# Squared-ReLU attention, a 2-D Fourier mix and a feed-forward block on one core: the whole kernel rebuilt around paired heads, folded DFT sums and another order of issue

## The chip, the core and the metric

The kernel runs on 1 core of one Trainium2 chip. The metric is device time in microseconds (us) of one execution; lower is better. A core has one matrix engine (TensorE, PE in the profile; PEld is its loading of weights), a vector engine (VectorE, DVE), an activation engine (ScalarE, ACT), GpSimd (POOL) and SyncE (SP), which each work through their own queue of instructions in order, and 16 DMA engines that move data between DRAM and the on-chip memory SBUF. Matrix products land in PSUM, eight banks of 512 fp32 words per partition.

## The reference, cut to what matters

```python
# q, k, v: (8, 12, 448, 64)   w_ch1: (768, 3072)   w_ch2: (3072, 768)
scores = (1 / sqrt(64)) * q @ k.T                  # per batch and head: 448 x 448
attn   = maximum(scores, 0) ** 2 / 448
x      = (attn @ v), heads side by side            # (8, 448, 768)
mixed  = real(fft(fft(x, axis=1), axis=2))         # over tokens, then over channels
u      = x + mixed
un     = (u - mean(u)) / sqrt(var(u) + 1e-6)       # over the 768 channels
out    = u + maximum(un @ w_ch1, 0) @ w_ch2        # (8, 448, 768), fp32
```

## The kernel before, in words

The eight batches are worked through one after the other, by a Python loop over `b`. Tokens are cut into four chunks of 112 (`SC = 4`, `SP = 112`), channels into six of 128 (`MC = 6`), the hidden layer into 24 of 128 (`JC = 24`).

- Loads. `load_qkv` fetches q, k and v of a batch with 12 DMAs from GpSimd's queue, which also turn fp32 into bf16. The weights (30 DMAs, L120 and L125) are issued ahead of the first of them.
- `transpose_qk` turns q and k on TensorE (L97, L103); ACT and DVE copy the results out of PSUM.
- Attention. For each head and each key chunk: a score product (L146, 64 rows of the array), Relu on ACT into the tile `rsc`, of which there is one (L149), the square on DVE (L150), and the product with v (L153, 64 columns of the array). The output of a head is scaled into `xT` (L155).
- Fourier mix. `x` is turned back to rows (L164). The channel DFT uses full cosine and sine matrices over 385 of 768 output columns (L177, L181), the token DFT full 448-square ones (L191, L193); the other 383 columns follow by symmetry (L200, on GpSimd). `u` stays in SBUF.
- Normalisation and feed-forward. `un` is made per token chunk (L211 to L223), turned (L227), multiplied with w1 (L235, 448 tokens at a time), passed through Relu on ACT (L237), multiplied with w2 (L245, 112 tokens by 384 channels, 24 products to a sum), and added to `u` (L247).

Each engine's order is set by the Tile framework's scheduler, which interleaves what the program order and the tile buffers allow; a tile with `bufs=n` can be in use n times at once.

Of the kernel before, what the change touches and what calls it, by code (L numbers as in the profile page):

```python
# [8 lines left out]
FP32 = mybir.dt.float32  # L10
# [6 lines left out]
def build_dft(nc, pool, psum_pool, nrows, N, ncols, phase_num, zero_t, chunk=128, prefix='dft'):  # L17
    import math
    tiles = []
    nchunks = (nrows + chunk - 1) // chunk  # L20
    for ci in range(nchunks):
        p0 = ci * chunk
        p = min(chunk, nrows - p0)
        rowidx = pool.tile([p, 1], I32)
        nc.gpsimd.iota(rowidx, pattern=[[0, 1]], base=p0, channel_multiplier=1)
        rowf = pool.tile([p, 1], FP32)
        nc.vector.tensor_copy(rowf, rowidx)
        colidx = pool.tile([p, ncols], I32)
        nc.gpsimd.iota(colidx, pattern=[[1, ncols]], base=0, channel_multiplier=0)
        colf = pool.tile([p, ncols], FP32)  # L30
        nc.vector.tensor_copy(colf, colidx)
        prod = pool.tile([p, ncols], FP32)
        nc.vector.tensor_scalar(prod, colf, rowf, None, op0=ALU.mult)
        off = N // 4 if phase_num == 0 else 0
        y = pool.tile([p, ncols], FP32)
        nc.vector.tensor_scalar(y, prod, 1.0 / N, float(off) / N, op0=ALU.mult, op1=ALU.add)
        r = pool.tile([p, ncols], FP32)
        nc.vector.tensor_scalar(r, y, float(2 ** 23), None, op0=ALU.add)
        nc.vector.tensor_scalar(r, r, float(2 ** 23), None, op0=ALU.subtract)
        d = pool.tile([p, ncols], FP32)  # L40
        nc.vector.tensor_tensor(d, y, r, op=ALU.subtract)
        t = pool.tile([p, ncols], BF16, name=f'{prefix}_{ci}')
        nc.scalar.activation(t, d, AF.Sin, bias=zero_t[:p], scale=2.0 * math.pi)
        tiles.append(t)
    return tiles
# [3 lines left out]
def kernel(  # L49
# [13 lines left out]
    SC = 4  # L63
    SP = S // SC
    MC = D // 128
    JC = FF // 128
    NC2 = 385
# [4 lines left out]
    attn_pool = ctx.enter_context(tc.tile_pool(name="attn", bufs=1))  # L72
    psum = ctx.enter_context(tc.psum_pool(name="ps", bufs=1))

    q_nat = [attn_pool.tile([SP, D], BF16, name=f'qn{_i}') for _i in range(SC)]
    k_nat = [attn_pool.tile([SP, D], BF16, name=f'kn{_i}') for _i in range(SC)]
    v_nat = [attn_pool.tile([SP, D], BF16, name=f'vn{_i}') for _i in range(SC)]
    qT_all = [attn_pool.tile([128, S], BF16, name=f'qT{_i}') for _i in range(MC)]
    kT_all = [attn_pool.tile([128, S], BF16, name=f'kT{_i}') for _i in range(MC)]

    def load_qkv(b):
        for c in range(SC):
            sl = slice(c * SP, (c + 1) * SP)
            nc.gpsimd.dma_start(out=q_nat[c].rearrange('p (h d) -> p h d', h=H),
                                in_=q[b, :, sl, :].rearrange('h p d -> p h d'))
            nc.gpsimd.dma_start(out=k_nat[c].rearrange('p (h d) -> p h d', h=H),
                                in_=k[b, :, sl, :].rearrange('h p d -> p h d'))
            nc.gpsimd.dma_start(out=v_nat[c].rearrange('p (h d) -> p h d', h=H),  # L88
                                in_=v[b, :, sl, :].rearrange('h p d -> p h d'))

    def transpose_qk():
        for c in range(SC):
            sl = slice(c * SP, (c + 1) * SP)
            for m in range(MC):
                msl = slice(m * 128, (m + 1) * 128)
                pt = psum.tile([128, SP], BF16, tag='p0', bufs=2)
                nc.tensor.transpose(pt, q_nat[c][:, msl], ident[:SP, :SP])  # L97
                if m % 2 == 0:
                    nc.scalar.activation(qT_all[m][:, sl], pt, AF.Copy)
                else:  # L100
                    nc.vector.tensor_copy(qT_all[m][:, sl], pt)
                pt2 = psum.tile([128, SP], BF16, tag='p1', bufs=2)
                nc.tensor.transpose(pt2, k_nat[c][:, msl], ident[:SP, :SP])  # L103
                if m % 2 == 0:
                    nc.vector.tensor_copy(kT_all[m][:, sl], pt2)  # L105
                else:
                    nc.scalar.activation(kT_all[m][:, sl], pt2, AF.Copy)

    ident = const.tile([128, 128], BF16)
    make_identity(nc, ident)  # L110
    import math as _m
    zero_t = const.tile([128, 1], FP32)
    nc.gpsimd.memset(zero_t, 0.0)
    eps_t = const.tile([128, 1], FP32)
    nc.gpsimd.memset(eps_t, 1e-6)

    w1_sb = []
    for m in range(MC):
        t = wpool.tile([128, FF], BF16, name=f'w1_{m}')
        nc.gpsimd.dma_start(out=t, in_=moe_w_ch1[m * 128:(m + 1) * 128, :])  # L120
        w1_sb.append(t)
    w2_sb = []
    for j in range(JC):
        t = wpool.tile([128, D], BF16, name=f'w2_{j}')
        nc.gpsimd.dma_start(out=t, in_=moe_w_ch2[j * 128:(j + 1) * 128, :])  # L125
        w2_sb.append(t)

    CD = build_dft(nc, const, psum, D, D, NC2, 0, zero_t, prefix='CD')
    SD = build_dft(nc, const, psum, D, D, NC2, 1, zero_t, prefix='SD')
    CS = build_dft(nc, const, psum, S, S, S, 0, zero_t, chunk=SP, prefix='CS')  # L130
    SS = build_dft(nc, const, psum, S, S, S, 1, zero_t, chunk=SP, prefix='SS')

    load_qkv(0)
    transpose_qk()

    for b in range(B):
        xT = [work.tile([128, S], BF16, name=f'xT{_i}') for _i in range(MC)]
        attnT = [attn_pool.tile([SP, S], BF16, name=f'attnT{_i}') for _i in range(SC)]
        for h in range(H):
            mt = h // 2  # L140
            rof = (h % 2) * Dh
            qT_h = qT_all[mt][rof:rof + Dh, :]
            kT_h = kT_all[mt][rof:rof + Dh, :]
            for c in range(SC):
                ps_sc = psum.tile([SP, S], FP32, tag='p2', bufs=2)
                nc.tensor.matmul(ps_sc, lhsT=kT_h[:, c * SP:(c + 1) * SP], rhs=qT_h,  # L146
                                 start=True, stop=True)
                r = attn_pool.tile([SP, S], BF16, name='rsc')
                nc.scalar.activation(r, ps_sc, AF.Relu, scale=1.0 / 8.0)  # L149
                nc.vector.tensor_tensor(attnT[c], r, r, op=ALU.mult)  # L150
            ps_ao = psum.tile([Dh, S], FP32, tag='p3', bufs=2)
            for kc in range(SC):
                nc.tensor.matmul(ps_ao, lhsT=v_nat[kc][:, h * Dh:(h + 1) * Dh],  # L153
                                 rhs=attnT[kc], start=(kc == 0), stop=(kc == SC - 1))
            nc.scalar.activation(xT[mt][rof:rof + Dh, :], ps_ao, AF.Copy, scale=1.0 / S)  # L155

        if b + 1 < B:
            load_qkv(b + 1)

        x_nat = [attn_pool.tile([SP, D], BF16, name=f'xnat{_i}') for _i in range(SC)]  # L160
        for c in range(SC):
            for m in range(MC):
                pt = psum.tile([SP, 128], BF16, tag='p0', bufs=2)
                nc.tensor.transpose(pt, xT[m][:, c * SP:(c + 1) * SP], ident)  # L164
                if m % 2 == 0:
                    nc.scalar.activation(x_nat[c][:, m * 128:(m + 1) * 128], pt, AF.Copy)
                else:
                    nc.vector.tensor_copy(x_nat[c][:, m * 128:(m + 1) * 128], pt)

        A_sb = [work.tile([SP, NC2], BF16, name=f'Asb{_i}') for _i in range(SC)]  # L170
        B_sb = [work.tile([SP, NC2], BF16, name=f'Bsb{_i}') for _i in range(SC)]
        for c in range(SC):
            nsl = slice(c * SP, (c + 1) * SP)
            psA = psum.tile([SP, NC2], FP32, tag='p2', bufs=2)
            psB = psum.tile([SP, NC2], FP32, tag='p3', bufs=2)
            for m in range(MC):
                nc.tensor.matmul(psA, lhsT=xT[m][:, nsl], rhs=CD[m],  # L177
                                 start=(m == 0), stop=(m == MC - 1))
            nc.scalar.activation(A_sb[c], psA, AF.Copy)
            for m in range(MC):  # L180
                nc.tensor.matmul(psB, lhsT=xT[m][:, nsl], rhs=SD[m],  # L181
                                 start=(m == 0), stop=(m == MC - 1))
            nc.scalar.activation(B_sb[c], psB, AF.Copy)
# [20 lines left out]
        if b + 1 < B:  # L204
            transpose_qk()
# [73 lines left out]
```

## Time and profile before

| | |
|---|---|
| median of 3 runs | 1318.64 us (1317.91 to 1319.39) |
| the profiled execution, its span | 1317.1 us |
| instructions | 13229 |
| mean granted TensorE clock | 0.795 of full speed |
| read from DRAM, written | 51.90 MB, 11.01 MB |

The profiled execution lasted as long as its span, from the first instruction to the last; what lies around the span is the 1.5 us between it and the median. A line of the profile's groups reads: line of the kernel, engine, operation, output <- input by the program's names, partitions x elements and type, count | busy us, mean ns of one | idle us of the engine just before them, and what ended most of it. Durations of matrix products include their way through the array; the distance between the starts of two is what a stream of them costs.

### The profile page before, as it was taken

How to read it: one execution, taken by the hardware profiler on the slowest of the kernel's cores; microseconds unless marked ns; L12 is line 12 of the kernel's file. 1: busy time of each engine (PE TensorE's matmuls, PEld its weight loads, DVE VectorE, ACT ScalarE, POOL GpSimd, SP SyncE). 2: the span in 40 equal slices, each digit the busy share in tenths (PEclk: the TensorE clock that was granted, in tenths of full speed). 3: DMA queues.
4: the chain of work that ended last, by engine and by line, in shares of the span. 5: the costliest groups of instructions: out<-in, count | busy, mean ns of one | idle time of the engine just before them, and what ended most of it. 6: DMA issues, size and time to landing. Idle time of an engine off the chain costs nothing.

```text
span 1317.1 us, 13229 instructions
## 1 busy us (share of the span) xinstructions
PE 1134.0 (86%) x4864; PEld 582.0 (44%) x4864; DVE 414.9 (31%) x1196; ACT 529.2 (40%) x1302; POOL 171.1 (13%) x238
## 2 busy tenths in 40 slices
PE   0139979998899979999799988999799997999698
PEld 0012436525473345624365254733456244642456
DVE  0694340235113360133402351133601334023501
ACT  0236552364415543164423644055431645236440
POOL 3740120003000130001200030001300010000100
PEclk9999969857796569957698577965699576975799
DMA  9980360105410360103601063103601030000001
GB/s 188 151 53 1 21 43 11 32 1 38 26 31 11 22 43 0 43 0 21 43 11 31 0 41 23 32 11 21 43 1 42 0 22 0 14 30 0 1 1 42
DMA packets 137505, 37.82 MB, mean 29 GB/s; under 512 B 131552, under 2 KB 134624, under 8 KB 137440
## 3 DMA queue, kind: packets, MB, share of 16 engines
q0 software_dynamic: 137440, 36.97, 26.2%
q8 instruction: 38, 0.62, 0.2%
q14 instruction: 27, 0.22, 0.1%
HBM read 51.90 MB, written 11.01 MB: 48 GB/s over the span
## 4 chain that ended last, share of the span: by engine, by line
PE 71%; DVE 10%; issue 8%; ACT 5%; DMA 3%; POOL 2%; POOLq 0%; ACTq 0%
PE pch L245 17%; PE ph L235 16%; PE ps_sc L146 13%; PE ps_ao L153 12%; PE psB L181 3%; PE psA L177 3%; DMA w<-in_moe_w_ch_dram 3%; ACT rsc L149 3%; DVE usb L202 2%; PE pt L164 2%; PE pt L227 2%; POOL usb L200 2%; DVE attnT L150 2%; PE pt L97 2%; DVE Qsb L198 1%
## 5 line engine op out<-in xcount | busy, mean ns | idle before, releaser
L149 ACT ACTIVATE rsc<-ps_sc 112x448 bf16<-112x448 f32 x384 | 208.1, 542 | 360.9 <-PE ps_sc L146 219.3
L245 PE MATMUL pch<-w,hT 128*112 128x384 bf16 x1536 | 250.9, 326 | 0.0
L235 PE MATMUL ph<-unT,w 128*128 128x448 bf16 x1152 | 240.3, 372 | 0.0
L150 DVE TENSOR_TENSOR attnT<-rsc 112x448 bf16<-112x448 bf16 x384 | 150.4, 392 | 244.9 <-ACT rsc L149 241.6
L153 PE MATMUL ps_ao<-attnT,vn 112*64 112x448 bf16 x384 | 214.3, 558 | 15.3 <-DVE attnT L150 11.7
L146 PE MATMUL ps_sc<-qT,kT 64*112 64x448 bf16 x384 | 208.3, 546 | 16.9 <-ACT rsc L149 13.6
L245 PEld LDWEIGHTS <-hT 128*112 128x112 bf16 x1536 | 199.7, 130 | 50.6
L247 DVE TENSOR_TENSOR o_sb<-pch,usb 112x384 f32<-112x384 f32 x64 | 35.7, 557 | 464.8 <-PE pch L245 436.5
L235 PEld LDWEIGHTS <-w 128*128 128x128 bf16 x1152 | 117.6, 102 | 120.5 <-issue 26.0
L237 ACT ACTIVATE hT<-ph 128x448 bf16<-128x448 f32 x192 | 104.5, 544 | 125.2 <-PE ph L235 125.2
L146 PEld LDWEIGHTS <-kT 64*112 64x112 bf16 x384 | 60.9, 160 | 144.1 <-issue 138.9
L153 PEld LDWEIGHTS <-vn 112*64 112x64 bf16 x384 | 48.0, 125 | 163.9 <-issue 163.9
L97 PE MATMUL pt<-ident,qn 112*128 112x112 bf16 x192 | 45.4, 261 | 73.0 <-DMA qn<-in_q_dram 51.0
L248 POOL DMA_DIRECT2D out_dram<-o_sb x32 | 17.4, 545 | 545.2 <-DVE o_sb L247 545.2
L88 POOL DMA_DIRECT2D vn<-in_v_dram x32 | 30.5, 952 | 372.2 <-PE ps_ao L153 371.4
L227 PE MATMUL pt<-ident,un 112*128 112x112 bf16 x192 | 41.8, 268 | 39.5 <-DVE un L223 25.4
L155 ACT ACTIVATE xT<-ps_ao 64x448 bf16<-64x448 f32 x96 | 51.4, 536 | 45.8 <-PE ps_ao L153 41.2
L103 PE MATMUL pt<-ident,kn 112*128 112x112 bf16 x192 | 43.6, 268 | 28.2 <-DVE kT L105 12.8
L97 PEld LDWEIGHTS <-qn 112*128 112x128 bf16 x192 | 21.8, 116 | 91.1 <-DMA qn<-in_q_dram 52.3
L228 ACT ACTIVATE unT<-pt 128x112 bf16<-128x112 bf16 x192 | 43.7, 262 | 36.0 <-PE pt L227 35.9
L181 PE MATMUL psB<-SD,xT 128*112 128x385 bf16 x192 | 54.3, 373 | 0.0
L200 POOL TENSOR_TENSOR usb<-Psb,Qsb 112x383 f32<-112x383 f32 x32 | 31.9, 996 | 166.2 <-DVE Qsb L198 141.1
(58 smaller groups left out, 826.9 us busy)
## 6 DMA issues: line engine op xcount, KB each, us to landing
out_dram<-o_sb POOLq DMA_DIRECT2D x32, 336.0 KB, 3.0
qn<-in_q_dram POOLq DMA_DIRECT2D x32, 168.0 KB, 4.6
kn<-in_k_dram POOLq DMA_DIRECT2D x32, 168.0 KB, 4.5
vn<-in_v_dram POOLq DMA_DIRECT2D x32, 168.0 KB, 3.9
w<-in_moe_w_ch_dram POOLq DMA_DIRECT2D x6, 768.0 KB, 14.6
w<-in_moe_w_ch_dram POOLq DMA_DIRECT2D x24, 192.0 KB, 7.3
```

The source lines that it names most:

```text
L97: nc.tensor.transpose(pt, q_nat[c][:, msl], ident[:SP, :SP])
L146: nc.tensor.matmul(ps_sc, lhsT=kT_h[:, c * SP:(c + 1) * SP], rhs=qT_h, start=True, stop=True)
L149: nc.scalar.activation(r, ps_sc, AF.Relu, scale=1.0 / 8.0)
L150: nc.vector.tensor_tensor(attnT[c], r, r, op=ALU.mult)
L153: nc.tensor.matmul(ps_ao, lhsT=v_nat[kc][:, h * Dh:(h + 1) * Dh], rhs=attnT[kc], start=(kc == 0), stop=(kc == SC - 1))
L155: nc.scalar.activation(xT[mt][rof:rof + Dh, :], ps_ao, AF.Copy, scale=1.0 / S)
L181: nc.tensor.matmul(psB, lhsT=xT[m][:, nsl], rhs=SD[m], start=(m == 0), stop=(m == MC - 1))
L200: nc.gpsimd.tensor_tensor(u_sb[c][:, NC2:D], P_sb[:, 383:0:-1], Q_sb[:, 383:0:-1], op=ALU.add)
L227: nc.tensor.transpose(pt, un[:, m * 128:(m + 1) * 128], ident[:SP, :SP])
L235: nc.tensor.matmul(ph, lhsT=w1_sb[m][:, jsl], rhs=unT[m], start=(m == 0), stop=(m == MC - 1))
L237: nc.scalar.activation(hT[j], ph, AF.Relu)
L245: nc.tensor.matmul(pch, lhsT=hT[j][:, csl], rhs=w2_sb[j][:, hsl], start=(j == 0), stop=(j == JC - 1))
```

## The change

What it does, part by part:

- **Loads.** A DMA carries four heads of q, k or v; tokens are read in neighbouring pairs, so pieces are 512 bytes in DRAM and not 256. DVE re-orders q and k (`qr`, `kr`, L80) so that chunks 0 and 1 hold the even tokens, 2 and 3 the odd ones. Order on GpSimd's queue: q, k, v of batch 0, half of w1, batch 1, the other half, w2 (4 DMAs for 24); then the IOTAs of the DFT tables.
- **Attention.** Two heads go together: their score products lie on rows 0 to 63 and 64 to 127 of the array and write two banks of one PSUM tile (L195), one Relu of 900 elements on ACT (L198, without the 1/8) and one square on DVE (L200) serve both, the products with v write partitions 0 to 63 and 64 to 127 (L202). `rsc` has 2 buffers, `sq` 3. The query columns are laid out so that two of the four chunks stand in reverse and with a zero column each: 450 columns for 448 queries.
- **Fourier mix.** Sums and differences of mirrored tokens (`xs`, `xa`) and of the two channel halves (`yp`, `ym`) replace the full matrices: 24 products of 225 columns (L236) and 24 of 193 (L253) per batch, for 48 and 32 of 385 before.
- **Residual.** `u` is written to a DRAM tensor `usc` by SP (L284, L292; reversed rows after a STREAM_SHUFFLE on DVE, L288) and read back per 128 tokens in the feed-forward (L347).
- **Feed-forward.** Over groups of 384 and 512 tokens instead of batches of 448, with 128-token tiles in the second product: 168 products of 384 columns per batch on average (L352) for 192 before. `ubot`, `o`, `psF` and `psA` have 2, 2, 2 and 3 buffers; the scratch `urev` shares the tag `o` with the feed-forward's output tile.
- **Order.** Attention and mix of batch b+2 (`front`) are issued ahead of the feed-forward of group b.

```diff
+    def psA(dtype=FP32):
+        n = 512 if dtype == FP32 else 1024
+        return psum.tile([128, 2, n], dtype, name="psA", tag="A", bufs=3)
+    def psF():
+        return psum.tile([128, 512], FP32, name="psF", tag="F", bufs=2)
...
+    def attention(b, tiles):
...
+            nc.vector.tensor_copy(qa, pq[:, 0:2, :])
+            nc.vector.tensor_copy(qb, pq[:, 2:4, ::-1])
+            nc.vector.tensor_copy(kT, pt[:, 1, 0:S])
+            av = psA()
+            for c in range(4):
+                sc = psA()
+                for e in range(2):
+                    ps = slice(e * Dh, (e + 1) * Dh)
+                    nc.tensor.matmul(sc[:R, e, 0:NQ], lhsT=kT[ps, c * R:(c + 1) * R], rhs=qT[ps, 0:NQ],
+                                     start=True, stop=True)
+                r = work.tile([R, 2, NQ], BF16, name="rsc", tag="rsc", bufs=2)
+                nc.scalar.activation(r, sc[:R, :, 0:NQ], AF.Relu)
+                s = work.tile([R, 2, NQ], BF16, name="sq", tag="sq", bufs=3)
+                nc.vector.tensor_tensor(s, r, r, op=ALU.mult)
+                for e in range(2):
+                    nc.tensor.matmul(av[e * Dh:(e + 1) * Dh, 0, 0:NQ], lhsT=vn[:, c, h0 + e, :],
+                                     rhs=s[:, e, :], start=(c == 0), stop=(c == 3))
+            x = work.tile([128, NQ], BF16, name="xT", tag=f"xT{m}", bufs=1)
+            nc.vector.tensor_scalar(x, av[:, 0, 0:NQ], 1.0 / (64.0 * S), None, op0=ALU.mult)
...
+    def mix(b, xT, seq, chan, unT):
...
+                if i == 0:
+                    nc.sync.dma_start(out=usc[row:row + R, :], in_=u[0:R, :])
+                else:
+                    w = work.tile([128, D], FP32, name="urev", tag="o", bufs=2)
+                    nc.vector.stream_shuffle(w, u, list(range(31, -1, -1)))
+                    for qd in range(4):
+                        lo, hi = max(n - R, 32 * qd), min(n, 32 * qd + 32)
+                        p0 = 64 * qd + 32 - hi
+                        nc.sync.dma_start(out=usc[row + n - hi:row + n - lo, :],
+                                          in_=w[p0:p0 + hi - lo, :])
...
+    def ffn(T0, N, unT):
...
+            nc.scalar.activation(h[:, 0:N], ph[:, 0:N], AF.Relu)
...
+        for c in range(N // 128):
+            t0 = T0 + c * 128
+            o = work.tile([128, D], FP32, name="o", tag="o", bufs=2)
+            nc.sync.dma_start(out=o, in_=usc[t0:t0 + 128, :])
+            for half in range(2):
+                hs = slice(half * (D // 2), (half + 1) * (D // 2))
+                pc = psF()
+                for j in range(JC):
+                    nc.tensor.matmul(pc[:, 0:D // 2], lhsT=hT[j][:, c * 128:(c + 1) * 128],
+                                     rhs=w2_sb[j // 6][:, j % 6, hs], start=(j == 0), stop=(j == JC - 1))
+                nc.vector.tensor_tensor(o[:, hs], pc[:, 0:D // 2], o[:, hs], op=ALU.add)
...
+    loaded = {0: load_qkv(0)}
+    load_w1(0)
+    loaded[1] = load_qkv(1)
+    load_w1(1)
+    load_w2()
+    seq, chan = build_dft()
...
+    front(0)
+    front(1)
+    for b in range(B):
+        if b + 2 < B:
+            front(b + 2)
+        ffn(*groups[b])
```

How the order on the engines moves. TensorE, in the middle of a batch's attention, before (`ps_sc` is a score tile, `ps_ao` the sum over key chunks):

```order
L153 MATMUL ps_ao_781<-attnT1_706,vn1_79 64x448
L146 LDWEIGHTS kT1_89
L146 MATMUL ps_sc_787<-qT1_83,kT1_89 112x448
L153 LDWEIGHTS vn2_80
L153 MATMUL ps_ao_781<-attnT2_707,vn2_80 64x448
L146 LDWEIGHTS kT1_89
L146 MATMUL ps_sc_792<-qT1_83,kT1_89 112x448
```

The same place in the change, at the start of a head pair (`psA_352` the first score tile, `psA_361` the second, `psA_351` the sum with v):

```order
L195 MATMUL psA_352<-qT2_92,kT_347 112x450
L202 LDWEIGHTS vn_112
L202 MATMUL psA_351<-sq_357,vn_112 64x450
L202 LDWEIGHTS vn_112
L202 MATMUL psA_351<-sq_357,vn_112 64x450
L195 LDWEIGHTS kT_347
L195 MATMUL psA_361<-qT2_92,kT_347 112x450
```

Before, a score product stands between any two products with v, and three of them run ahead at the start of a batch. Now the first product with v of a pair stands between the first and the second score tile; the other three score tiles follow behind it.

TensorE where one feed-forward ends, before: the whole feed-forward stands ahead of the next attention.

```order
L245 LDWEIGHTS hT22_1553
L245 MATMUL pch_1936<-w2_22_159,hT22_1553 112x384
L245 LDWEIGHTS hT23_1554
L245 MATMUL pch_1936<-w2_23_161,hT23_1554 112x384
L146 LDWEIGHTS kT0_88
L146 MATMUL ps_sc_1973<-qT0_82,kT0_88 112x448
```

In the change, in the attention of batch 1 (`psF` is a tile of the feed-forward's first product, group 0):

```order
L195 MATMUL psA_808<-qT0_88,kT_803 112x450
L339 LDWEIGHTS w1_4_0_132
L339 MATMUL psF_1909<-unT_576,w1_4_0_132 128x384
L339 LDWEIGHTS w1_5_0_134
L339 MATMUL psF_1909<-unT_576,w1_5_0_134 128x384
L339 LDWEIGHTS w1_4_0_132
L339 MATMUL psF_1918<-unT_576,w1_4_0_132 128x384
```

Here products of the feed-forward stand between the steps of a head pair. Along the whole queue this holds for the first product of groups 0, 2 and 4 (beside the attention of batches 1, 4 and 6) and for 48 products of the second one in each of groups 0 to 5; the attention of batches 0 and 2, four of six head pairs in batches 3, 5 and 7, and every mix but for those 48 products have no feed-forward between them, and groups 6 and 7 stand alone at the end.

DVE at the end of the mix of batch 2, in the change (`un` is the normalised input, `o` the output tile of group 0, `psF` its sums):

```order
L304 TENSOR_SCALAR un_1872<-u_1846,rstd_1868,nmr_1870 112x768
L304 TENSOR_SCALAR un_1874<-ubot1_77,rstd_1868,nmr_1870 112x768
L354 TENSOR_TENSOR o_2125<-psF_2127,o_2125 128x384
L354 TENSOR_TENSOR o_2125<-psF_2153,o_2125 128x384
L354 TENSOR_TENSOR o_2181<-psF_2183,o_2181 128x384
```

Before, the two `L247` additions of a token chunk followed its products at once:

```order
L223 TENSOR_SCALAR un_1511<-usb3_1184,rstd_1506,nmr_1508 112x768
L247 TENSOR_TENSOR o_sb_1747<-pch_1748,usb0_1181 112x384
L247 TENSOR_TENSOR o_sb_1747<-pch_1774,usb0_1181 112x384
L247 TENSOR_TENSOR o_sb_1801<-pch_1802,usb1_1182 112x384
```

The first addition of group 0 has moved behind the mix of batch 2, and so has every later product of that sum: `psF` has two buffers, and the two finished halves of the first token tile fill them.

438 lines of the change are left out of this document (248 added, 190 removed).

## The prediction

> **What bounds the kernel now.** I read the windows first (busy time per engine and granted clock), then the chain that ended last, then the timeline of one attention step, then the groups by line and shape for prices, last the start of GpSimd's queue.
>
> The windows: PE, PEld, DVE, ACT, POOL busy, granted clock, DMA share, GB/s.
>
> ```profile
> 216.00:246.00 30.00, 30.00 (x186) 24.02 (x185) 3.90 (x7) 0.00 (x0) 1.64 (x3) 1.00 0.11 35
> 252.00:297.00 45.00, 44.30 (x87) 12.64 (x86) 15.95 (x42) 27.72 (x54) 0.00 (x0) 0.50 0.00 1
> 321.00:340.00 19.00, 12.49 (x71) 6.98 (x71) 12.66 (x51) 10.47 (x49) 8.48 (x9) 0.50 1.14 72
> 340.00:368.00 28.00, 28.00 (x139) 13.99 (x138) 0.00 (x0) 12.73 (x24) 0.00 (x0) 0.93 0.00 1
> ```
>
> The stages take turns: attention (252 to 297) has 87 products in 45 us at half clock, the two feed-forward products (340 to 368, then as 216 to 246) are dense at 0.93 and 1.00. The chain gives their lengths:
>
> ```profile
> 186.79 28.40 PE ph L235 x141
> 215.19 31.20 PE pch L245 x192
> 246.74 0.55 ACT rsc L149
> ...
> 339.92 28.63 PE ph L235 x141
> 368.55 31.20 PE pch L245 x192
> ```
>
> One batch is 339.92 - 186.79 = 153.1 us: 60 us feed-forward, the rest attention and mix. In an attention step no engine is full:
>
> ```profile
> 261.85 0.54 ACT L149 ACTIVATE rsc<-ps_sc 112x448 bf16<-112x448 f32 x1 [0.52 <-DVE attnT L150]
> 262.43 0.39 DVE L150 TENSOR_TENSOR attnT<-rsc 112x448 bf16<-112x448 bf16 x1 [0.67 <-ACT rsc L149]
> 262.92 0.54 ACT L149 ACTIVATE rsc<-ps_sc 112x448 bf16<-112x448 f32 x1 [0.52 <-DVE attnT L150]
> ```
>
> ACT waits for DVE's square to free the one `rsc`, DVE for ACT: 1.07 us per head and key chunk, 8.5 us for the eight steps of two heads. The hand-over costs 0.04 to 0.10 us; I use 0.07.
>
> **Prices.** Groups by line and shape:
>
> ```profile
> L149 ACT ACTIVATE rsc<-ps_sc 112x448 bf16<-112x448 f32 x384 | 208.1, 542 | 360.9 <-PE ps_sc L146 219.3 <-DVE attnT L150 140.3
> L150 DVE TENSOR_TENSOR attnT<-rsc 112x448 bf16<-112x448 bf16 x384 | 150.4, 392 | 244.9 <-ACT rsc L149 241.6 <-PE ps_ao L153 3.1
> L146 PE MATMUL ps_sc<-qT,kT 64*112 64x448 bf16 x384 | 208.3, 546 | 16.9 <-ACT rsc L149 13.6
> L228 ACT ACTIVATE unT<-pt 128x112 bf16<-128x112 bf16 x192 | 43.7, 262 | 36.0 <-PE pt L227 35.9
> L97 PEld LDWEIGHTS <-qn 112*128 112x128 bf16 x192 | 21.8, 116 | 91.1 <-DMA qn<-in_q_dram 52.3 <-issue 34.4
> L105 DVE COPY kT<-pt 128x112 bf16<-128x112 bf16 x96 | 20.2, 210 | 2.3 <-PE pt L103 2.0
> L200 POOL TENSOR_TENSOR usb<-Psb,Qsb 112x383 f32<-112x383 f32 x32 | 31.9, 996 | 166.2 <-DVE Qsb L198 141.1 <-DVE mv L214 13.9 <-DVE qT L101 9.6
> L202 DVE TENSOR_TENSOR usb<-usb,xnat 112x768 f32<-112x768 f32 x32 | 30.5, 954 | 8.9 <-POOL usb L200 8.8
> L223 DVE TENSOR_SCALAR un<-usb,rstd,nmr 112x768 bf16<-112x768 f32 x32 | 22.0, 687 | 16.3 <-PE pt L227 16.3
> L199 DVE TENSOR_TENSOR usb<-psP,Qsb 112x385 f32<-112x385 f32 x32 | 17.7, 555 | 1.2 <-ACT std L216 0.3
> L212 DVE BATCH_NORM_STATS2 stats<-usb 112x6 f32<-112x384 f32 x32 | 17.6, 549 | 0.0
> L214 DVE BATCH_NORM_AGGREGATE mv<-stats 112x2 f32<-112x12 f32 x32 | 6.4, 200 | 0.0
> L220 DVE TENSOR_TENSOR nmr<-mv,rstd 112x1 f32<-112x1 f32 x32 | 4.9, 154 | 0.5
> L183 ACT ACTIVATE Bsb<-psB 112x385 bf16<-112x385 f32 x32 | 15.8, 495 | 7.3 <-PE psB L181 7.3
> L216 ACT ACTIVATE std<-mv,eps_t 112x1 f32<-112x1 f32 x32 | 9.2, 288 | 10.7 <-DVE mv L214 10.7
> ```
>
> ACT: (542 - 262)/336 = 0.83 ns an element, so a Relu of 900 costs 0.92 us and one of 384 0.49. DVE: 154 ns for one element; the bf16 square adds 0.53 ns an element, so 0.63 us for 900; fp32 adds 1.04 (L202 against L199). Copies of `kT` (448) cost 0.38 and of each q half (224) 0.27 at the slope from 1 to 112 elements (L220, L105), 0.62 and 0.39 at the fp32 slope; I take the first, which L105 itself gives. `xT` (450, fp32) 0.62. A transpose costs its weight load, 116 ns.
>
> **Attention by itself, per head pair.** Half the instructions do twice the work, and `rsc` has two buffers, so ACT alone would need 4 x 0.92 = 3.7 us. But TensorE works in order, and there the first product with v stands ahead of score tiles 2 to 4. In us from the first score product: scores there 0.55, Relu 0.62 to 1.54, square to 2.23, first product with v 2.30, second score tile only now, to 3.22; Relus 2, 3, 4 end at 4.20, 5.12, 6.04. The next pair's transposes need the PSUM tile that Relu 3 frees: 5.34 to 6.44. Then on DVE, every other pair: q copy, fourth square (7.40), q copy and `kT` to 8.05; next score product 8.1. In the pairs between, two re-ordering copies (1024 elements, 0.70 each) come ahead of the fourth square and `xT` ahead of `kT`: 9.6. Mean 8.85 us, 53 per batch. That is no less than the 8.5 plus scaling of before: the wait on the one `rsc` has become a wait of TensorE for the first square. Bounds: copies at twice the bf16 rate 8.5, heads that don't share the array 9.9 (448 columns at half clock are 2 x 0.1625 x 448/384 = 0.38, with the dense price below; 0.35 to 0.38 more at three places).
>
> The Trainium skill ("TensorEngine Tiling (Array Packing)", Key Properties) says that different tiles run in parallel but that changing the tiling mode drains the array. No run shown here has two heads at once. By the rows a drain is about 0.17 us (L146's 0.546 less those 0.38), hidden in a lone attention where TensorE waits anyway, but beside the feed-forward 8 changes per pair would add 1.4 us to each of 18 pairs, 25 us in all: 1050 instead of the sum below.
>
> **Attention beside the first product.** 24 products of 384 columns per pair, each 201 ns (28.4/141) x 384/448 = 0.173, fill the two waits of TensorE. At full clock the same walk gives 8.75 and 7.4 us, mean 8.2: 49 per batch, and the 25 us of the feed-forward cost nothing. If the cover goes, 25 x 3 comes back.
>
> **The mix**, summed along its chain: last transposes 1.2; copies of `x` (1536 bf16) 2 x 0.95; four bf16 sums of 768, 0.56 each, 2.25; first `y` 0.6; three times ACT 0.54, two DVE passes of 0.62 and hand-overs, 5.8; products and `qs` 2.25 (L183); then DVE for both halves: four `tpm` and four `u` at 0.555, eight statistics at 0.55, four aggregates, two STREAM_SHUFFLEs (no row; I take L202's 0.95, between 0.69 of L223 and twice L202), two `un` of 0.69 and the two small steps: 13.2; std and the rest 0.7; two `un` 1.4; products and Relu-free copy 2.1. Total 32 us; 37 with copies and bf16 sums at the fp32 slope and slow shuffles, 30 with all three at half their price. GpSimd's part (L200, 2.0 us a half) lies beside DVE's statistics. Before, 153.1 less 60 and 48 x 1.07 leaves 42 for this stretch and the transposes of q and k.
>
> **Feed-forward alone.** Second product 31.20/192 = 0.1625 us each; first 0.173 at 384 columns and 0.230 at 512.
>
> **Start.** GpSimd's queue, and the row of the second weight's DMAs (count, KB each, us to landing):
>
> ```profile
> 1.36 0.70 POOL L120 DMA_DIRECT2D w<-in_moe_w_ch_dram  x1 [0.35 <-issue]
> ...
> 42.49 0.53 POOL L125 DMA_DIRECT2D w<-in_moe_w_ch_dram  x1 [0.39 <-DMA w<-in_moe_w_ch_dram]
> ...
> w<-in_moe_w_ch_dram POOLq DMA_DIRECT2D x24, 192.0 KB, 7.3
> ```
>
> 9.4 MB of weights took from 1.4 to 49.8 us, 195 GB/s. q, k and v of batch 0 now come first: attention starts near 11 us (memsets to 3, three issues, a landing of some 4); before, its first Relu of the chain stood at 101.6:
> ```profile
> 101.59 0.55 ACT rsc L149
> ```
>
> The table IOTAs (0.5 us each) stand behind the last weight DMA, which goes out once the eighth before it has landed: by then 4.3 MB of w1 and 3.4 MB of q, k, v, 40 us at this rate, so near 46. Attention needs five pairs, to 55, before DVE comes to the tables: no wait. Tables on DVE: 9600 elements in 22 operations, 12 us. Attention 0 ends at 76, its mix at 108. The residual's DMAs stand on SP's empty queue; a load lies behind the mix's stores but has 7.8 us of products (48 x 0.1625) per 128 tokens as cover. If it had none, see the last rival.
>
> **The sum**, by the order of TensorE: 108; batch 1: 49 + 32 = 81; batch 2: 53 + 32 = 85 (the feed-forward stands still, since its second product waits for an `o` tile that the mix holds); group 0's remaining 96 products 15.6, group 1's first product 33.2, batch 3 53 + 32: 134. Batches 4 and 6 each: 3 + 144 products 23.4 + 46.7 beside + 32 = 105; batches 5 and 7 each 134. Then groups 5 to 7 alone: 23.4 + 24.9 + 23.4 + 33.2 + 31.2 = 136; last addition and store 4. Total 108 + 81 + 85 + 134 + 2 x 239 + 136 + 4 = 1026 us against the profiled 1317.1, itself 1.5 below the median: 1027.
>
> **The rivals.**
> - *The heads of a pair don't share the array* (or each change of mode drains it). For it: half clock in attention, and no row of two heads at once. Against: TensorE waits there in any case. 30 pairs by themselves x 1.05 = 32, 18 beside x 1.5 = 27: 1085.
> - *Steps are shorter than I walked*: 8.3 and 7.6 us per pair, mixes of 29 and a dense clock earlier: 30 x 0.55 + 18 x 0.6 + 8 x 3 + 8 = 59: 968.
> - *No gain in attention and none from the cover*: the products between the steps delay the chain instead of filling it, 75 us back: 1101.
> - *The bounced residual ends it slower.* If every 128-token tile waited bare for its store and load on SP, 28 tiles would pay. It decides above 292/28 = 10.4 us each; at 12 the time is 1363. For it: two `o` buffers shared with the mix's scratch. Against: a 336 KB store landed in 3.0 us:
>
> ```profile
> out_dram<-o_sb POOLq DMA_DIRECT2D x32, 336.0 KB, 3.0
> ```
>
> **How the numbers follow.** My walk 0.50 (its own range 990 to 1065), array not shared 0.20, shorter steps 0.17, lost cover 0.10, bare residual 0.02, a mishap under no name 0.01. With the array not shared and mixes of 37 us the first two reach 1120; below, shorter steps with their own spread reach 935: the range. The measurement of this kernel tells apart about 0.2%; faster 0.97, same 0.01, slower 0.02.
>
> **What would show it.** Right: groups L198 and L200 near 0.92 and 0.63 us; attention of batch 2 near 53 us with ACT busy 40% and TensorE waiting for `sq`; the first product absent from the chain in batches 1, 4 and 6; a last stretch of 136 us of dense products. Wrong: idle TensorE ahead of L352 that ends with a DMA (residual), pairs whose products with v start 0.37 us apart (array not shared), mixes over 37 us, a DVE stall at the tables after 60 us.

## The result, and the profile after

The changed kernel takes 1024.45 us (median of four, 1023.38 to 1025.28) against 1319.02 us (1317.91 to 1319.96) for the kernel before on the same chip: a ratio of 0.7764, interval 0.7753 to 0.7775. The forecast was 1027 us. The profiled execution has a span of 1022.4 us at a mean granted clock of 0.824 (before 0.795).

The page of the changed kernel: busy time of TensorE and ACT, and the granted clock in 40 equal slices.

```profile
PE 766.5 (75%) x4404; PEld 406.9 (40%) x4416; DVE 413.4 (40%) x862; ACT 324.8 (32%) x484; POOL 117.3 (11%) x139
...
PEclk9996998556599656999799756799979955699999
```

No engine is full. The windows of its stages say where TensorE is, in the columns of the windows before: the attention of batch 1 (104 to 154), that of batch 2 (183 to 237), the mix of batch 2 (238 to 268).

```profile
104.00:154.00 50.00, 48.84 (x311) 22.76 (x309) 25.08 (x54) 32.91 (x52) 6.68 (x9) 0.99 0.38 38
...
183.00:237.00 54.00, 32.52 (x152) 13.93 (x149) 24.68 (x53) 22.26 (x26) 6.55 (x8) 0.50 0.35 34
238.00:268.00 30.00, 12.86 (x83) 9.85 (x84) 21.35 (x44) 3.61 (x8) 6.10 (x5) 0.61 0.25 54
```

With feed-forward products between its steps an attention keeps TensorE 98% busy at a clock of 0.99, and takes no longer than one that has the array to itself at 0.50: 50 us against 55. The chain that ended last gives the rest (start, length, what; L339 is the first feed-forward product, L352 the second):

```profile
14.75 0.93 ACT rsc L198
...
104.52 1.66 PE psF L339 x7
...
259.36 7.98 DMA usc<-urev
267.36 3.05 DMA o<-usc
271.21 18.16 PE psF L352 x96
289.64 10.74 PE psF L339 x49
...
511.10 17.69 PE psF L352 x96
750.39 17.51 PE psF L352 x96
882.65 25.74 PE psF L352 x144
```

Two rows ahead of 271.21 are no products: a store of the mix's scratch `urev` that lands 7.98 us after its issue, and the load of the residual tile `o`, which is issued 0.02 us after that. The groups show the same wait as L352's idle time, and the two steps that the attention chain consists of:

```profile
L352 PE MATMUL psF<-w,hT 128*128 128x384 bf16 x1344 | 239.5, 336 | 11.8 <-DVE o L354 11.8
L198 ACT ACTIVATE rsc<-psA 112x900 bf16<-112x900 f32 x192 | 168.9, 918 | 220.5 <-PE psA L195 220.5
L200 DVE TENSOR_TENSOR sq<-rsc 112x900 bf16<-112x900 bf16 x192 | 120.3, 626 | 172.1 <-ACT rsc L198 172.1
L202 PE MATMUL psA<-sq,vn 112*64 112x450 bf16 x384 | 93.5, 475 | 63.1 <-DVE sq L200 61.8
```

ACT waits 220.5 us for score products, TensorE 61.8 for squares. TensorE's timeline of one head pair that has the array to itself shows how (start, length, line, count, idle time before and what ended it):

```profile
14.09 0.62 PE L195 MATMUL psA<-qT,kT 64*112 64x450 bf16 x2 [2.67 <-DVE kT L189]
16.39 0.59 PE L202 MATMUL psA<-sq,vn 112*64 112x450 bf16 x2 [1.68 <-DVE sq L200]
16.90 1.00 PE L195 MATMUL psA<-qT,kT 64*112 64x450 bf16 x4
...
23.59 0.62 PE L195 MATMUL psA<-qT,kT 64*112 64x450 bf16 x2 [1.02 <-DVE kT L189]
```

After the first score tile TensorE stands still for 1.68 us, since its next instruction is a product with v that needs the first square; score tiles 2 and 3 follow only behind that. The next pair begins 9.50 us after this one.

### The profile page after: what moved, and what is told of

The parts are those of the page before. It is cut to its first block, busy times and chain, and to the rows that moved or that the text cites. A ratio compares the mean times of both kernels' runs of the same rounds, so it can differ in the third digit from the quotient of the medians.

```text
span 1022.4 us, 11062 instructions
## 1 busy us (share of the span) xinstructions
PE 766.5 (75%) x4404; PEld 406.9 (40%) x4416; DVE 413.4 (40%) x862; ACT 324.8 (32%) x484; POOL 117.3 (11%) x139
## 4 chain that ended last, share of the span: by engine, by line
PE 65%; DVE 17%; ACT 9%; DMA 5%; issue 2%; POOL 0%; SPq 0%; ACTq 0%; DVEq 0%; POOLq 0%
PE psF L352 21%; PE psF L339 21%; PE psA L202 7%; ACT rsc L198 7%; PE psA L195 7%; DVE sq L200 3%; DMA usc<-urev 3%; PE psA L179 2%; PE psA L218 2%; DVE stats L280 2%; PE psA L236 2%; PE psA L253 2%; DMA o<-usc 1%; PE psA L180 1%; DVE u L276 1%
## 5 line engine op out<-in xcount | busy, mean ns | idle before, releaser
L352 PE MATMUL psF<-w,hT 128*128 128x384 bf16 x1344 | 239.5, 336 | 11.8 <-DVE o L354 11.8
L198 ACT ACTIVATE rsc<-psA 112x900 bf16<-112x900 f32 x192 | 168.9, 918 | 220.5 <-PE psA L195 220.5
L339 PE MATMUL psF<-unT,w 128*128 128x384 bf16 (+1 forms) x1140 | 237.1, 354 | 1.6 <-ACT hT L342 0.6
L200 DVE TENSOR_TENSOR sq<-rsc 112x900 bf16<-112x900 bf16 x192 | 120.3, 626 | 172.1 <-ACT rsc L198 172.1
L352 PEld LDWEIGHTS <-hT 128*128 128x128 bf16 x1344 | 133.4, 101 | 106.5 <-issue 29.7
L342 ACT ACTIVATE hT<-psF 128x384 bf16<-128x384 f32 (+1 forms) x192 | 104.0, 543 | 215.5 <-PE psF L339 214.4
L339 PEld LDWEIGHTS <-w 128*128 128x128 bf16 x1152 | 107.5, 98 | 114.6 <-issue 21.3
L202 PE MATMUL psA<-sq,vn 112*64 112x450 bf16 x384 | 93.5, 475 | 63.1 <-DVE sq L200 61.8
L354 DVE TENSOR_TENSOR o<-psF,o 128x384 f32<-128x384 f32 x56 | 30.6, 556 | 228.3 <-PE psF L352 212.4
L195 PE MATMUL psA<-qT,kT 64*112 64x450 bf16 x384 | 88.7, 494 | 37.2 <-DVE kT L189 18.0
L202 PEld LDWEIGHTS <-vn 112*64 112x64 bf16 x384 | 29.2, 118 | 118.4 <-issue 83.6
L195 PEld LDWEIGHTS <-kT 64*112 64x112 bf16 x384 | 32.6, 154 | 87.7 <-issue 54.3
L179 PE MATMUL psA<-ident,qr 112*128 112x112 bf16 x192 | 32.5, 254 | 8.4 <-DVE qr L80 8.0
L180 PE MATMUL psA<-ident,kr 112*128 112x112 bf16 x192 | 32.8, 256 | 2.3 <-DVE kr L80 2.3
```

What stands on the lines that cost most here:

```text
L179: nc.tensor.transpose(pt[:, 0, c * R:(c + 1) * R], qn[:, c, hs], ident[:R, :R])
L180: nc.tensor.transpose(pt[:, 1, c * R:(c + 1) * R], kn[:, c, hs], ident[:R, :R])
L195: nc.tensor.matmul(sc[:R, e, 0:NQ], lhsT=kT[ps, c * R:(c + 1) * R], rhs=qT[ps, 0:NQ], start=True, stop=True)
L198: nc.scalar.activation(r, sc[:R, :, 0:NQ], AF.Relu)
L200: nc.vector.tensor_tensor(s, r, r, op=ALU.mult)
L202: nc.tensor.matmul(av[e * Dh:(e + 1) * Dh, 0, 0:NQ], lhsT=vn[:, c, h0 + e, :], rhs=s[:, e, :], start=(c == 0), stop=(c == 3))
```

## The experiments

Times are medians on the chip; the kernel before had medians of 1320.74, 1319.01 and 1319.33 us beside the three groups of runs. Ratios are to it, with their intervals.

### Score product ahead of the product with v

```diff
-            av = psA()
+            av = None
+            done = []
...
-                for e in range(2):
-                    nc.tensor.matmul(av[e * Dh:(e + 1) * Dh, 0, 0:NQ], lhsT=vn[:, c, h0 + e, :],
-                                     rhs=s[:, e, :], start=(c == 0), stop=(c == 3))
+                done.append(s)
+                for cc in ([] if c == 0 else [c - 1] if c < 3 else [2, 3]):
+                    if av is None:
+                        av = psA()
+                    for e in range(2):
+                        nc.tensor.matmul(av[e * Dh:(e + 1) * Dh, 0, 0:NQ], lhsT=vn[:, cc, h0 + e, :],
+                                         rhs=done[cc][:, e, :], start=(cc == 0), stop=(cc == 3))
```

> Edit: in attention the score product of the next key chunk is written ahead of the product with v of the chunk before, so TensorE's queue holds two score tiles ahead of the first product with v. Theory (a lone head pair is bound by the place of the first product with v on TensorE's queue): a lone pair falls from 8.8 us to about 7.7 (walk: second Relu right behind the first, at 1.54), one beside the feed-forward from 8.0 to about 7.5; 30 x 1.05 + 18 x 0.5 = 40 us, so about 984 us. Rival (the pair is bound by its engines or by the copies on DVE): within 5 us of 1024.

Measured: 985.06 us (983.89 to 986.58), ratio 0.746 (0.7447 to 0.7472), 39 us less than the change. The same place of TensorE's timeline (L196 the score product, L207 the product with v):

```profile
13.99 1.00 PE L196 MATMUL psA<-qT,kT 64*112 64x450 bf16 x4 [3.00 <-DVE kT L189]
16.39 0.59 PE L207 MATMUL psA<-sq,vn 112*64 112x450 bf16 x2 [1.40 <-DVE sq L201]
16.91 0.99 PE L196 MATMUL psA<-qT,kT 64*112 64x450 bf16 x3
...
22.73 1.00 PE L196 MATMUL psA<-qT,kT 64*112 64x450 bf16 x4 [1.02 <-DVE kT L189]
```

Two score tiles now stand ahead of the wait, and the next pair begins after 8.74 us instead of 9.50. So in a lone pair it is the place of that one product in TensorE's queue that binds, as the prediction's walk had it. A pair beside the feed-forward fell too, from 8.02 to 7.24 us in batch 1, but there most of the gain is work placed elsewhere: from the first `xT` scaling to the last the trace has 110 feed-forward products instead of 130 (20 x 0.1625 over five pairs is 0.65 a pair), and the others stand in the mix, which takes 31.0 us as before.

### The scratch of the mix on a tag of its own

```diff
-                s = work.tile([R, 2, NQ], BF16, name="sq", tag="sq", bufs=3)
+                s = work.tile([R, 2, NQ], BF16, name="sq", tag="sq", bufs=2)
...
-                    w = work.tile([128, D], FP32, name="urev", tag="o", bufs=2)
+                    w = work.tile([128, D], FP32, name="urev", tag="urev", bufs=1)
```

> Edit: the reversed-row scratch urev gets one buffer of its own and leaves the two buffers of tag o to the feed-forward; sq has 2 buffers for 3, to make the room. Theory (the second product stands still in lone attention and mix only because its o tile is held by the mix): the feed-forward now runs beside all of batches 1 to 7; 104 us start, 7 x (50 + 31 to 34), some 112 us of feed-forward alone at the end and 4: 800 to 830 us. Rival (the shared tag costs only the bare waits of second product on the residual's load, 11.8 us in the trace): 1012 us.

Measured: 799.70 us (799.35 to 801.41), ratio 0.6056 (0.6047 to 0.6065): 225 us less than the change. Its page, its group of second products, and its windows (attention of batch 2, mix of batch 2, attention of batch 3):

```profile
PE 702.3 (88%) x4397; PEld 360.9 (45%) x4416; DVE 411.4 (52%) x862; ACT 322.3 (40%) x484; POOL 115.8 (15%) x139
...
PEclk9999999999999999999999999999999999999999
...
L352 PE MATMUL psF<-w,hT 128*128 128x384 bf16 x1344 | 256.2, 330 | 2.5 <-DVE o L354 2.5
```

```profile
188.00:238.00 50.00, 48.69 (x285) 20.13 (x289) 25.80 (x56) 32.13 (x44) 6.57 (x8) 1.00 0.47 63
238.00:268.00 30.00, 26.92 (x175) 15.70 (x174) 22.66 (x47) 7.29 (x14) 6.62 (x5) 0.94 0.25 54
268.00:319.00 51.00, 50.41 (x338) 24.15 (x337) 27.20 (x60) 26.45 (x36) 6.55 (x8) 1.00 0.59 99
```

In the order of instructions, the attention of batch 2 had no feed-forward product between its steps in the change and has 131 here, the mix of batch 2 now 109, the attention of batch 3 160. The stages are no longer than before; what went is the time between them, in which the feed-forward stood alone. With `urev` and `o` on one tag, every mix lies between two users of `o` in that ring of two, so the second product of group 0 cannot go on past its first token tile before the mix of batch 2 is done. The wait for the residual (11.8 us) shrinks to 2.5 with it, and the clock stays at 0.99. The single `urev` has a price of its own: DVE waits 12.1 us, in eight places, until the store before has landed.

### Two buffers for `sq` alone

```diff
-                s = work.tile([R, 2, NQ], BF16, name="sq", tag="sq", bufs=3)
+                s = work.tile([R, 2, NQ], BF16, name="sq", tag="sq", bufs=2)
```

> The changed kernel with two buffers instead of three for `sq`, and nothing else: it separates the two halves of own_scratch, which gave `urev` a tag of its own and took one `sq` buffer away to make room. The order of instructions on every engine is the same as in the changed kernel. Theory (the shared tag `o` alone held the second product back): the third buffer is idle, since a square is read by its two products with v before the one after next is written; 1024 us, 1020 to 1029. Rival (the smaller `sq` ring has a part in own_scratch's 224 us): below 1015. Other rival (the ring of two is a stall of its own that own_scratch paid for): above 1030.

Measured: 1024.07 us (1022.78 to 1025.12), ratio 0.7756 (0.7739 to 0.7774), the time of the change. The 225 us are the tag's alone.

### No look-ahead

```diff
-    front(0)
-    front(1)
     for b in range(B):
-        if b + 2 < B:
-            front(b + 2)
+        front(b)
         ffn(*groups[b])
```

> Edit: front(b) is followed by ffn of group b, no front is issued ahead. TensorE's queue then holds attention, mix and feed-forward strictly one after the other. Theory (the cover is worth what it hides: 3 first products of 24 us, 6 x 48 second products of 0.1625 = 47 us, less 12 us of waits on the residual that go): 104 + 7 x (53 + 30) + 4 x 110 + 4 = about 1130 us. Rival (products between the steps delay the chain as much as they hide, the lost-cover rival): within 20 us of 1024.

Measured: 1151.42 us (1149.96 to 1152.64), ratio 0.8715 (0.8702 to 0.8728). The cover is worth 127 us. The change has 3 x 144 first products (0.173 us each) and 6 x 48 second ones (0.1625) beside other work, 75 + 47 = 122 us; the expectation fell short. Part of what is left is the slow start of each lone feed-forward, in its chain:

```profile
384.50 2.68 PE psF L339 x12
387.27 21.61 PE psF L339 x132
408.88 23.41 PE psF L352 x144
```

The first 12 products take 2.68 us, at the pace of the next 132 they would take 1.96.

### Heads that don't share the array

```diff
-                    nc.tensor.matmul(sc[:R, e, 0:NQ], lhsT=kT[ps, c * R:(c + 1) * R], rhs=qT[ps, 0:NQ],
+                    nc.tensor.matmul(sc[:R, e, 0:NQ], lhsT=kT[:, c * R:(c + 1) * R], rhs=qT[:, 0:NQ],
```

> Edit in the changed kernel: each of a pair's two score products takes all 128 rows of the array (both heads' rows of kT and qT), so the two can't share it; each head's scores become the sum of both heads'. Number, length and order of the instructions stay. Theory (the two products of a pair run side by side in the changed kernel): each pair of score products takes 0.38 us more of TensorE at half clock, 0.19 at full clock; on the chain of a lone pair that is the first score tile twice over and the later ones in part, 0.7 to 1.1 us a pair, beside the feed-forward 0.4 to 0.8: 30 x 0.9 + 18 x 0.6 = 38, so 1050 to 1075 us. Rival (they ran one after the other all along): 1024 within 5 us, or less by the changes of mode that fall away.

Measured: 1040.44 us (1039.38 to 1044.14), ratio 0.7894 (0.7877 to 0.791): 16 us more than the change, below the theory's range and above the rival's. TensorE's timeline at the same pair as above:

```profile
14.02 1.00 PE L195 MATMUL psA<-qT,kT 128*112 128x450 bf16 x2 [2.93 <-DVE kT L189]
16.69 0.58 PE L202 MATMUL psA<-sq,vn 112*64 112x450 bf16 x2 [1.67 <-DVE sq L200]
17.20 1.75 PE L195 MATMUL psA<-qT,kT 128*112 128x450 bf16 x4
```

Two score products take 1.00 us instead of 0.62, four 1.75 instead of 1.00: on all rows they go one behind the other, 0.38 us each; on halves of the rows a pair costs the time of one. So the heads do share the array in the change. What it is worth on the path is less than 0.38 at three places: from `xT` to `xT` a lone pair of batch 0 takes 9.45 us instead of 8.77 (mean of pairs 1 to 5), a pair beside the feed-forward in batch 1 8.24 instead of 8.02.

### The kernel before with two buffers for `rsc`, and with q, k, v and the tables ahead of the weights

```diff
-                r = attn_pool.tile([SP, S], BF16, name='rsc')
+                r = attn_pool.tile([SP, S], BF16, name='rsc', tag='rsc', bufs=2)
```

> The kernel before, with two buffers for rsc instead of one, nothing else. Theory (the step of 1.07 us was the hand-over between Relu and square through the one buffer): the step falls to what its engines need: ACT 0.54 + a quarter of 0.54 = 0.68; TensorE two streams of 448 columns and two changes of mode of 0.13, 1.0 us at half clock or 0.64 at full. So between 384 x 0.07 = 27 and 384 x 0.37 = 142 us less: 1177 to 1292 us, and which end tells whether the half clock holds it. Rival (TensorE bound the step, not the buffer): 1319 within 5 us.

Measured: 1217.99 us (median of five, 1192.76 to 1222.63), between 0.904 and 0.927 of the kernel before. In the profiled run, which is the fastest, ACT's wait for the square falls from 140.3 us to 8.9:

```profile
L149 ACT ACTIVATE rsc<-ps_sc 112x448 bf16<-112x448 f32 x384 | 199.0, 541 | 271.4 <-PE ps_sc L146 251.5 <-DVE attnT L150 8.9 <-DVE r L38 0.2
```

What holds the step now is TensorE's product (251.5), and the step did not fall everywhere. Windows of the attention of batch 2 and of batch 3:

```profile
370.00:415.00 45.00, 44.75 (x97) 13.14 (x96) 18.53 (x49) 30.88 (x62) 0.74 (x2) 0.58 0.03 8
516.00:548.00 32.00, 30.85 (x101) 11.23 (x100) 18.83 (x51) 29.17 (x62) 1.12 (x2) 1.00 0.04 12
```

In batches 1, 3, 6 and 7 a step takes 0.63 us (score products of TensorE start at 521.61 and 522.24). In batch 2 it takes 1.06 (381.81 and 382.87), as with one buffer, and TensorE is busy 44.75 of 45 us at a clock of 0.58. So the one `rsc` was not the only bound of the old step: at half pace TensorE's two products take just as long. The five runs, at 1192.76, 1208.37, 1217.99, 1220.52 and 1222.63 us, had mean clocks of 0.885, 0.867, 0.856, 0.855 and 0.853. The buffer is worth 96 to 126 us, presumably by the number of batches that reach full pace, which was read in one run only.

```diff
+    load_qkv(0)
+    CD = build_dft(nc, const, psum, D, D, NC2, 0, zero_t, prefix='CD')
...
     w1_sb = []
...
-    CD = build_dft(nc, const, psum, D, D, NC2, 0, zero_t, prefix='CD')
...
-    load_qkv(0)
```

> The kernel before, with q, k and v of batch 0 loaded first, then the DFT tables and last the weights; nothing else. Theory (of the time won, some 60 to 85 us is the start: attention at 14 us and not at 101): the tables, 90 small operations on DVE, stay ahead of much of the attention, so 45 to 70 us less: 1250 to 1275 us. Rival (weights are needed as early as before, so the wait moves to the first feed-forward): 1310 to 1319 us.

Measured: 1274.58 us (1274.26 to 1275.02), ratio 0.9664 (0.965 to 0.9678): 44 us less. In the chain the first feed-forward stands at 142.80 instead of 186.79. In the changed kernel it stands at 104.52, so the order of the loads, tried in the old kernel, is worth 44 of these 82 us. The old tables still stand in the way of the first attention: DVE is busy 37.45 of the 40 us from 20 to 60.

### Both edits together, and the score product ahead in batch 0 only

Both edits of the first two experiments:

> Both edits together. Theory: beside the feed-forward a pair is bound by TensorE's own work (24 products of 0.17, 8 transposes, 16 products that pair up, about 7 us), so 0.5 to 1 us of 8 is gained per pair over own_scratch: 20 to 40 us less, 770 to 800 us. Rival (with the feed-forward in the gaps the order of scores no longer matters): the same as own_scratch within 5 us.

Measured: 813.07 us (810.53 to 813.35), ratio 0.615 (0.614 to 0.616), slower than the new tag alone: a miss. Starts of the `xT` scaling (us) of each batch's first and last pair, from the timelines of DVE:

| batch | the change | own tag | both edits |
|---|---|---|---|
| 1 | 113.5, 153.6 | 116.4, 156.5 | 111.3, 147.5 |
| 2 | 193.0, 237.2 | 197.1, 237.8 | 187.5, 223.5 |
| 4 | 439.0, 479.0 | 359.0, 399.7 | 338.5, 375.5 |
| 5 | 569.2, 612.5 | 446.1, 486.4 | 447.4, 485.2 |
| 7 | 808.3, 848.7 | 626.3, 664.5 | 635.8, 673.5 |

The attentions did get faster, in batch 4 37.0 us from the first `xT` to the last instead of 40.8. But between the last pair of batch 4 and the first of batch 5 stand 71.9 us instead of 46.4, since the scheduler placed all 144 first products of a group there, with nothing beside them:

```profile
407.78 10.74 PE psF L344 x49
418.57 10.74 PE psF L344 x49
429.37 9.44 PE psF L344 x43
```

A shorter pair leaves less room for covered products: in the trace the attention of batch 4 holds 127 of them, and 146 with the new tag alone. The rest has to go somewhere, with TensorE 88% busy. That this alone makes up the 13 us was not tested. So the edit was kept where no feed-forward exists to fill with:

```diff
+                for cc in ([c] if b else [] if c == 0 else [c - 1] if c < 3 else [2, 3]):
```

> own_scratch, with the scores written ahead in batch 0 alone, the one batch whose attention has no feed-forward beside it. Theory (the order of scores pays where TensorE has nothing else to do, 0.83 us for each of six pairs, and with the later batches' order untouched nothing is lost to denser stretches): 5 us less than own_scratch, 793 to 797 us. Rival (the start is bound by loads or tables instead): the same as own_scratch within 1 us.

Measured: 794.67 us (793.32 to 797.61), ratio 0.6028 (0.6014 to 0.6043), the best version here, 230 us less than the change. The gain of 5.0 us over the new tag alone is the earlier end of batch 0: its last `xT` starts at 65.29 instead of 71.98, 6.7 us.

## Why the prediction was right, point by point

**The sum.** Its milestones against the chain, in us:

| | predicted | measured |
|---|---|---|
| first product of the feed-forward | 108 | 104.52 |
| 96 second products of group 0 | 274 | 271.21 |
| the same two batches later | 513 | 511.10 |
| and again | 752 | 750.39 |
| feed-forward alone | 886 | 882.65 |
| end of the span | 1026 | 1022.4 |

All of the difference arises in the first stage, and there two errors cancel in part: the first score product stands at 14.09, not near 11, and the tables on DVE lengthen the sixth pair of batch 0 to 14.2 us, 5 more than a usual one and not 12. Two batches were to take 239 us and took 239.9 and 239.3; the last stretch 136 and took 134.9 (882.65 to the last addition at 1017.50). That these agree within 1 us is partly luck. Waits of some 3 us on the residual and 18.2 us for 96 second products (15.6 in the sum) stand against first products of 512 columns at 0.219 us (10.74/49; 0.230 in the sum) and mixes that are shorter than 32.

**Prices.** Relu 0.92 was 0.918, square 0.63 was 0.626, `kT` 0.38 was 0.381, q halves 0.27 were 0.273, `xT` 0.62 was 0.627, STREAM_SHUFFLE 0.95 was 0.994. The re-ordering copies were mis-sized, 0.70 against 0.441 and 0.420.

**Attention by itself.** Walked as 9.6 and 8.1 us, mean 8.85. Score products of batch 0 start at 14.09, 23.59, 31.57, 41.12 and 49.10, so 9.50, 7.98, 9.55 and 7.98; in batch 2 the mean from `xT` to `xT` is 8.85. The place of the wait was right, and an edit of nothing but that place gave 39 us. That the attention of the change is hardly faster than the old one was right too. The 9.5 of the long pair is in part luck: its two re-ordering copies were priced 0.54 us too dear together, but the first of them waits 0.63 us for transposes (DVE at 20.59), which the walk did not have.

**What bounded the old attention.** The prediction says that "no engine is full" there and puts the step of 1.07 us down to the one `rsc`. Its own window has TensorE busy 44.30 of 45 us, and with two buffers the step stayed at 1.06 in batch 2, where TensorE ran at half pace. Both held the step, and the reading named one. The sum does not use it.

**Beside the feed-forward.** Predicted 8.2, measured 8.02, but not as the walk had it. The walk let products fill two waits of TensorE and gave a change of tiling mode no price. What holds a pair here is TensorE itself, busy 48.84 of 50 us in the window above and on the chain with its feed-forward products. Its timeline in batch 1:

```profile
128.00 1.15 PE L339 MATMUL psF<-unT,w 128*128 128x384 bf16 x6
129.08 0.38 PE L202 MATMUL psA<-sq,vn 112*64 112x450 bf16 x2
129.39 1.48 PE L339 MATMUL psF<-unT,w 128*128 128x384 bf16 x8
130.80 0.40 PE L195 MATMUL psA<-qT,kT 64*112 64x450 bf16 x2
```

From start to start, six dense products and the change behind them take 1.08 us and eight take 1.41: 0.16 for a product, so 0.1 is left for the change. The two products with v hold the queue for 0.31 us, where 450 columns at the dense pace are 0.19 (0.1625 x 450/384): again 0.1. A pair has some 13 such changes, so about 1.2 of its 8.02 us go there by this estimate, close to the 1.4 that the prediction priced for the drain. That the pair took 8.02 all the same, and that the sum by the drain, 1050, did not come, suggests that the walk was too long elsewhere by about as much, which is luck. The Trainium skill ("TensorEngine Tiling (Array Packing)", Key Properties) states both that tiles run in parallel and that a change of mode drains the array. The trace agrees with the first (0.62 us for two score products, 1.00 where they can't share) and shows a cost at each change; no run separates the drain from the loading of weights.

**The mix.** Predicted 32; in batch 2 the stretch from the end of the last `xT` (237.9) to the mix's last product (268.5) is 30.6, and in batches 1, 4 and 6, with second products beside it, 28.3.

**The residual.** Here a step failed: a load "has 7.8 us of products (48 x 0.1625) per 128 tokens as cover". At four places, of 28 loads, the first load of a group has none. It gets its buffer from `urev`, whose store lands only 7.98 to 8.11 us after its issue, and lands 2.96 to 3.54 later: TensorE waits some 2.9 us each time, 11.8 in all. It doesn't show in the total, since the eight mixes were shorter than the 32 by 1.2 to 3.7 us each.

**The rivals.** That the heads don't share the array was right in its place and too dear: 1085 forecast, 1040 when it is forced. Lone pairs lose 0.7 us, not 1.05, and those beside the feed-forward 0.2, not 1.5. That the cover fails was refuted, and is dearer than the 75 us priced: 127, because second products are covered too. The bare residual is 3 us at 4 places, not 10.4 at 28. The steps were not shorter than walked.

**The signs.** One sign of being right did not come: "the first product absent from the chain in batches 1, 4 and 6". In batch 1 the chain holds at least 17 us of it, from 104.52 on, since TensorE is the limit there. One sign of being wrong did come, idle TensorE ahead of L352 that ends with a DMA, but it is the 11.8 us above.

**What it did not see.** It wrote that the feed-forward "stands still, since its second product waits for an `o` tile that the mix holds" and counted it, but did not ask what the shared tag costs. That was the largest term left in the kernel: 225 us, against 295 for the whole change.

**Where the 294.7 us between the two spans come from:** 82 lie ahead of the first feed-forward product (186.79 to 104.52), 126 come from the cover (1148.0 to 1022.4 without it), and 87, the rest, from the shorter mix and the fewer feed-forward products. No run splits the rest; 24 products less per batch at 0.1625 are an estimated 31 of it. The attention, by its pair times, gave nothing.

## What to carry to other kernels

Count the users of every buffer ring in the order of issue: a scratch tile that shares a tag with another stage's output ties the two stages together, and the profile shows little of it as a wait (11.8 us here) and most of it as stages in which TensorE has too little to do. Where TensorE works in order, put ahead of an instruction that must wait everything that needs not, but only while the engine has idle time to win: at 88% busy the same edit made this kernel slower. Before a wait between two engines is called the bound, look whether a third is full too. A store and load through DRAM held TensorE at 4 of 28 tiles here, the first of a group each time, for some 3 us.

## What the runs showed of the hardware

- **The granted clock did not tell the pace.** In the attention of batch 0 the window from 14 to 72 us has a granted clock of 1.00, and in batch 2 (183 to 237, above) 0.50:

```profile
14.00:72.00 58.00, 32.27 (x146) 13.67 (x146) 33.22 (x75) 26.13 (x30) 18.44 (x29) 1.00 1.31 203
```

  But TensorE's timeline has four score products in 1.00 us in both (16.90 above, and 196.76), and in 0.59 beside the feed-forward:

```profile
124.64 0.59 PE L195 MATMUL psA<-qT,kT 64*112 64x450 bf16 x4
...
196.76 1.00 PE L195 MATMUL psA<-qT,kT 64*112 64x450 bf16 x4
```

  After a mix the first 12 dense products take twice as long as 12 in batch 1, in the chain:

```profile
155.28 1.95 PE psF L352 x12
...
271.21 4.00 PE psF L352 x12
```

  The Trainium skill ("TensorE: Matmul & The Clock Gate", Part 1) says that half clock comes after an idle window of about 3.4 us and full clock after as long a busy one. The slow start of dense products agrees (96 in 18.16 us instead of 15.6, so 2.6 us lost); in batch 2 the clock stayed at 0.50 with waits of at most 1.8 us inside the pairs, which that rule alone doesn't give.
- **Two products share the array, and a change of tiling costs.** Two score products on halves of the rows take 0.62 us, on all rows 1.00; beside dense products a change costs about 0.1 us (above).
- **A store to DRAM can land late.** In the chain of the change the stores of `urev` (four DMAs, 336 KB together) landed 7.98 to 8.11 us after their issue, and 7.39 to 7.80 in that of the kernel with the new tag, where the 336 KB stores of the kernel before had a median of 3.0. Which of their shape, their queue and the neighbours makes the difference was not tried.
- **Sums of GpSimd and DVE that run side by side are longer.** Rows of the change by shape; 113 partitions is the first half of a batch, 112 the second:

```profile
L276 DVE TENSOR_TENSOR u<-tpm,xn 113x383 f32<-113x383 f32 x8 | 10.1, 1260 | 0.0
L275 DVE TENSOR_TENSOR u<-tpm,xn 113x385 f32<-113x385 f32 x8 | 8.1, 1014 | 0.0
L276 DVE TENSOR_TENSOR u<-tpm,xn 112x383 f32<-112x383 f32 x8 | 5.1, 634 | 0.0
...
L275 POOL TENSOR_TENSOR ubot<-tpm,xn 112x385 f32<-112x385 f32 x8 | 21.8, 2725 | 0.0
L275 POOL TENSOR_TENSOR ubot<-tpm,xn 113x385 f32<-113x385 f32 x8 | 9.8, 1224 | 0.0
```

  DVE's sums take up to twice as long in the first half as in the second, and where DVE's are short GpSimd's takes 2725 ns instead of 1224. The Trainium skill ("SBUF — State Buffer", SBUF: two separate sides) says that a DVE instruction with two SBUF inputs and one of GpSimd that reads SBUF exclude each other for the whole length of the one that starts first. These rows agree: in batch 2 DVE's second sum, begun at 254.14, ends 0.41 us after GpSimd's, which ran from 253.77 to 254.99. No run here took one of the two away.
